# Seven products of quarter sums for eight in two blocks of a two-layer float32 network on one Trainium2 core

## The chip, the cores and the metric

One core of one Trainium2 chip runs the whole program. The metric is the device time of one execution in microseconds, as the median of several runs. TensorE's clock was granted at full speed in every slice of the profile.

## The reference

An attention block with 32 state rows per head gives 2,176 rows of 512 numbers (17 tiles of 128 rows). Two expert layers follow, each of the form `g(x @ w_in) @ w_out` with widths 512, 2,048 and 512, all in float32:

```python
def _moe2_ref(x, w_in, w_out):
    h = x @ w_in
    sp = np.where(h > 20.0, h, np.log1p(np.exp(np.minimum(h, 20.0))))
    g = h * np.tanh(sp)
    return (g @ w_out).astype(np.float32)
```

The first layer has ELU in place of this function. The change concerns the second layer's last line, `g @ w_out`.

## The kernel before

**Products.** A float32 operand is split into a high part in the fast float32 format of TensorE and a low part that holds the rest. Each product is then three matmuls into one accumulator: high by high, high by low, low by high (lines 872 to 874 in the first product of a layer, 972 to 974 in the second). Each matmul loads its own 128x128 stationary operand and streams up to 512 columns.

**Steps.** The work is a list of steps. In the second layer, BLOCKS2 (line 39) makes five blocks of 4, 4, 4, 3 and 2 tiles; a block has 16 steps, one for each slice j of 128 of the 2,048 hidden columns. In a step of a block of four tiles `mm1` (line 839) issues 12 matmuls of 512 columns into one PSUM bank of the tag `h`, which has four banks (SPOTS). `hidden` (line 884) turns that bank into g on ScalarE and VectorE: Exp, a bound, a product, Ln, Exp, two products (lines 919 to 931), then the split into a high part by ScalarE and a low part by VectorE (`split_g`, line 934). Two steps later `mm2` (line 940) multiplies the four tiles of g by the slice of `w_out`, 12 matmuls of 512 columns, into the four banks acc0 to acc3, which add up over the 16 steps. `retire` (line 983) copies the accumulators out and stores them. The last two blocks ("narrow", line 1116) issue four steps of `mm1` and then four of `mm2`.

**Order.** Every instruction is added to a plan with a cost and due times from a table T of step starts (line 347). `Plan.run` (line 126) simulates the engines and always issues what can start first, ties going to what is due first; the result is a fixed order for each engine. A transfer is issued by SP's queue, in the order that the plan gave. Buffers come from pools of named tags with a fixed number of buffers, among them `w_out` (16), `wraw` (3), `o` (4), `e`, `g`, `u` and `ms` (2 each).

**Weights.** `weight` (line 460) brings the second layer's weights from 64-bit words to float32 and parks them in DRAM (w2d). `reload` (line 522) fetches them again and `split_weight` (line 515) splits them into the 16 `w_in` and 16 `w_out` buffers, where they stay for all five blocks. `fold_slice` (line 564) and the first layer are not touched.

Of the kernel before, what the change touches and what calls it, by code (L numbers as in the profile page):

```python
# [235 lines left out]
def attention_elu_mish(  # L236
# [41 lines left out]
    s2d = pools["dram"].tile([B, 2, P, S], F32, name="s2d")  # L278
    at = ctx.enter_context(ExitStack())
# [61 lines left out]
    def mm2_cost(kind, n, whole=False):  # L341
        return 4 * mm(4 * S) if whole else 12 * mm(n * P if kind == 1 else DM)
# [5 lines left out]
    for s, (kind, blk, t0, n, j) in enumerate(steps):  # L348
        c = mm1_cost(kind, blk, n, j) + (mm2_cost(kind, n, whole_out(kind, blk, j)) if kind < 2 else n * 3 * mm(DM))
        T.append(T[-1] + c + (PACE_FIRST if s < NF // 2 else PACE if s < first2 else 0.0))  # L350
# [171 lines left out]
    def reload(kind, j):  # L522
        v = buf("work", "wraw", 3, [P, DM], F32, f"back_{kind}_{j}_")
        add(SP, 256.0, lambda: nc.sync.dma_start(out=v.t, in_=w2d[:, kind == "out", j, :]),
            r=[("w2d", kind, j)], w=[v])
        split_weight(kind, 2, j, v)


# [355 lines left out]
    def hidden(s, h):  # L884

        kind, blk, t0, n, j = steps[s]
        e = buf("work", "e", EBUFS, [P, MAXN])
# [19 lines left out]
        if apart(s):  # L907
            g = buf("l2", "g", 2, [P, 2, n * P], F32R, "g")
        else:
            g = buf("work", "g", GBUFS, [P, 2, MAXN], F32R, "g")  # L910
        gs[s] = g
        last = s == len(steps) - 1
        g.parts = [(0, n // 2), (n // 2, n)] if last else [(0, n)]
        sw = switch
        for q, (c0, c1) in enumerate(g.parts):
# [16 lines left out]
            split_g(g, e, c0 * P, c1 * P, [ke], q)  # L932
# [7 lines left out]
    def mm2(s, only=None):  # L940
        kind, blk, t0, n, j = steps[s]
        g = gs[s]
        part = (kind, blk)
# [161 lines left out]
    for j in range(NF):  # L1105
        begin(index[1, 3, j], reload, "in", j)
        begin(min(index[1, 3, j] + 1, first2), reload, "out", j)
    for blk in range(len(BLOCKS2)):
        begin(first2 + NF * (blk - 1) + 6 if blk else s_state + NQ + 4, load_x2, blk)
# [8 lines left out]
    for s in range(len(steps) + 2):  # L1118
# [13 lines left out]
        if s < len(steps) and s >= narrow and (s - narrow) % GROUP < GROUP - 1:  # L1132
            held.append(s - 2)
            continue
# [55 lines left out]
SPOTS = 4  # L1190
WARM, EARLY, XB, EBUFS, GBUFS, FOLD_LAG = 14, 8, 3, 2, 2, 3.0
# [25 lines left out]
```

## Time and profile before

| | |
|---|---|
| median of 3 runs | 714.25 us (714.08 to 714.56) |
| the profiled execution's own time | 714.31 us |
| its span in the profile | 712.4 us |
| TensorE busy | 706.3 us of the span, 4,082 matmuls |
| VectorE busy | 526.1 us |
| ScalarE busy | 411.6 us |
| DMA | 81.50 MB, 114 GB/s on the mean |

PE is TensorE's matmul side, PEld its weight loads, DVE is VectorE, ACT ScalarE, SP the queue that issues transfers. Matmuls are pipelined, so that the duration of one is longer than the distance to the next: the pace is read from start times. Neighbouring instructions of VectorE and of ScalarE overlap a little in the same way. L972 is line 972 of the kernel.

### The profile page before, as it was taken

To read this page: it belongs to the slowest core of one execution; us is meant where nothing else is said; L and a number is where in the kernel's file an instruction comes from. 1 tells how busy PE (TensorE), PEld (TensorE's weight loads), DVE (VectorE), ACT (ScalarE), POOL (GpSimd) and SP (SyncE) were. 2 spreads that over 40 slices of the span, in tenths; PEclk is the share of its full clock that TensorE was granted. 3 is DMA by queue.
4 is the path that set the end of the run, shared out by engine and by line. 5 is a ranking of instruction groups with operands and counts; after the bars stand their busy time and mean duration, and the time that the engine had idled before them with its cause. 6 is when DMAs were issued, how large, how long until landed. Compare 5 with 4: busy or idle time off the path is not lost.

```text
span 712.4 us, 10844 instructions
## 1 busy us (share of the span) xinstructions
PE 706.3 (99%) x4082; PEld 583.2 (82%) x4082; DVE 526.1 (74%) x1004; ACT 411.6 (58%) x735; POOL 11.8 (2%) x26
## 2 busy tenths in 40 slices
PE   8999999999999999999999999999999999999998
PEld 7578777878888898788888888888888889999887
DVE  7999998879797846887888566666666647665575
ACT  4987775656666734565666455544545436554464
POOL 1000000100000000000000000000000000000000
PEclk9999999999999999999999999999999999999999
DMA  9846788364788835636860003000030000200100
GB/s 288 292 148 194 221 212 218 95 143 105 239 218 256 262 104 169 203 120 193 261 225 13 1 0 119 0 1 1 2 102 1 1 1 1 88 1 1 45 1 30
DMA packets 89895, 81.50 MB, mean 114 GB/s; under 512 B 46452, under 2 KB 68980, under 8 KB 89844
## 3 DMA queue, kind: packets, MB, share of 16 engines
q1 hardware_dynamic: 89428, 80.63, 37.9%
q8 instruction: 32, 0.52, 0.3%
q10 hardware_dynamic: 416, 0.20, 0.1%
q14 instruction: 19, 0.16, 0.1%
HBM read 59.31 MB, written 21.50 MB: 113 GB/s over the span
## 4 chain that ended last, share of the span: by engine, by line
PE 97%; DMA 1%; ACT 1%; DVE 0%; issue 0%; SPq 0%; DVEq 0%; ACTq 0%
PE acc_acc L972 17%; PE acc_acc L973 17%; PE acc_acc L974 17%; PE h L872 13%; PE h L873 13%; PE h L874 13%; PE fold L551 2%; PE h L848 2%; PE h L858 1%; DMA raw_in<-in_moe_w_in 1%; PE sr L796 1%; PE acc_acc L960 1%; PE acc_h L973 1%; PE acc_h L974 1%; PE acc_h L972 1%; PE warm L385 0%
## 5 line engine op out<-in xcount | busy, mean ns | idle before, releaser
L936 ACT CAST g<-e 128x512 fp32r<-128x512 f32 (+3 forms) x148 | 86.2, 582 | 119.9 <-DVE e L930 63.2
L937 DVE TENSOR_TENSOR g<-e,g 128x512 fp32r<-128x512 f32 (+3 forms) x148 | 95.1, 644 | 49.2 <-ACT g L936 48.1
L874 PE MATMUL h<-x,w_in 128*128 128x512 f32 (+2 forms) x320 | 114.2, 357 | 0.0
L873 PE MATMUL h<-x,w_in 128*128 128x512 f32 (+2 forms) x320 | 114.2, 357 | 0.0
L872 PE MATMUL h<-x,w_in 128*128 128x512 f32 (+2 forms) x320 | 114.2, 357 | 0.0
L972 PE MATMUL acc_acc<-w_out,g 128*128 128x512 f32 x272 | 106.0, 390 | 0.0
L973 PE MATMUL acc_acc<-w_out,g 128*128 128x512 f32 x272 | 105.9, 390 | 0.0
L974 PE MATMUL acc_acc<-w_out,g 128*128 128x512 f32 x272 | 105.9, 389 | 0.0
L972 PE MATMUL acc_acc<-g,w_out 128*128 128x512 f32 x252 | 100.2, 398 | 0.0
L973 PE MATMUL acc_acc<-g,w_out 128*128 128x512 f32 x252 | 98.2, 390 | 0.0
L974 PE MATMUL acc_acc<-g,w_out 128*128 128x512 f32 x252 | 98.1, 389 | 0.0
L924 ACT ACTIVATE e<-u,two 128x512 f32<-128x512 f32 (+3 forms) x81 | 53.0, 655 | 64.3 <-DVE u L922 64.1
L928 DVE TENSOR_TENSOR u<-u,e 128x512 f32<-128x512 f32 (+3 forms) x81 | 48.9, 605 | 53.6 <-ACT e L926 53.2
L919 ACT ACTIVATE e<-h 128x512 f32<-128x512 f32 (+3 forms) x81 | 42.7, 529 | 45.8 <-PE h L874 37.4
L872 PEld LDWEIGHTS h<-x,w_in 128*128 128x128 f32 x320 | 60.3, 189 | 7.8
L873 PEld LDWEIGHTS h<-x,w_in 128*128 128x128 f32 x320 | 60.3, 189 | 7.7
L874 PEld LDWEIGHTS h<-x,w_in 128*128 128x128 f32 x320 | 60.3, 188 | 7.5
L972 PEld LDWEIGHTS acc_acc<-w_out,g 128*128 128x128 f32 x272 | 51.1, 188 | 11.0 <-ACT o L294 0.5
L974 PEld LDWEIGHTS acc_acc<-w_out,g 128*128 128x128 f32 x272 | 51.1, 188 | 10.7
L891 ACT ACTIVATE e<-h 128x512 f32<-128x512 f32 x68 | 40.2, 595 | 33.7 <-PE h L874 22.4
L973 PEld LDWEIGHTS acc_acc<-w_out,g 128*128 128x128 f32 x272 | 51.1, 188 | 10.2
L920 DVE TENSOR_SCALAR e<-e 128x512 f32<-128x512 f32 (+3 forms) x81 | 31.0, 383 | 36.8 <-ACT e L919 36.0
(149 smaller groups left out, 1125.8 us busy)
## 6 DMA issues: line engine op xcount, KB each, us to landing
raw_in<-in_moe_w_in SPq DMA_DIRECT2D x32, 512.0 KB, 5.1
raw_out<-in_moe_w_out SPq DMA_DIRECT2D x32, 512.0 KB, 4.0
w2d<-wv SPq DMA_DIRECT2D x32, 256.0 KB, 3.3
x2d<-o SPq DMA_DIRECT2D x16, 256.0 KB, 3.5
xb<-in_x SPq DMA_DIRECT2D x32, 128.0 KB, 4.4
back_in<-w2d SPq DMA_DIRECT2D x16, 256.0 KB, 3.3
back_out<-w2d SPq DMA_DIRECT2D x16, 256.0 KB, 3.0
out<-o SPq DMA_DIRECT2D x15, 256.0 KB, 2.1
```

The costliest lines, as they stand in the source:

```text
L872: nc.tensor.matmul(h[:, :n], lhsT=wh, rhs=xh, start=(k == 0), stop=False)
L873: nc.tensor.matmul(h[:, :n], lhsT=wh, rhs=xl, start=False, stop=False)
L874: nc.tensor.matmul(h[:, :n], lhsT=wl, rhs=xh, start=False, stop=(k == nk - 1))
L891: add("ACT", act(n), lambda: nc.scalar.activation(E(), Hh(), AF.Exp), r=[h], w=[e])
L919: add("ACT", act(n), lambda c=c: nc.scalar.activation(e[:, c], h[:, c], AF.Exp), r=[h], w=[ke])
L924: add("ACT", act(n) + 0.1, lambda c=c: nc.scalar.activation(e[:, c], u[:, c], AF.Ln, bias=two), r=[ku, "two"], w=[ke])
L928: add("DVE", dve(n), lambda c=c: nc.vector.tensor_tensor(u[:, c], u[:, c], e[:, c], ALU.mult), r=[ku, ke], w=[ku])
L936: add("ACT", act(n), lambda: nc.scalar.copy(g[:, 0, c], e[:, c]), r=r, w=[(g, 0, q)])
L937: add("DVE", dve(n), lambda: nc.vector.tensor_tensor(g[:, 1, c], e[:, c], g[:, 0, c].bitcast(F32), ALU.subtract), r=[*r, (g, 0, q)], w=[(g ...
L972: nc.tensor.matmul(acc.t, lhsT=st[:, 0, :], rhs=mv[:, 0, :], start=fst, stop=False)
L973: nc.tensor.matmul(acc.t, lhsT=st[:, 0, :], rhs=mv[:, 1, :], start=False, stop=False)
L974: nc.tensor.matmul(acc.t, lhsT=st[:, 1, :], rhs=mv[:, 0, :], start=False, stop=lst)
```

## The change

In blocks 1 and 2 of the second layer (`SEVEN`) two neighbouring slices j of the hidden columns make a pair, eight pairs to a block. g of the pair (512 rows by 256 columns) and the two slices of `w_out` (256 by 512) are each cut into four quarters, and the 2x2 product of quarters is made in seven products of sums of quarters. One product is 6 matmuls of 256 columns; its accumulator fills a bank of its own through the eight pairs: acc0 to acc3 and three of the four banks of `h`.

- `hidden` copies the bank of `h` to SBUF first (ScalarE), and reads the copy from then on.
- `g_sums` makes four sums of quarters of g on VectorE for each pair, and splits seven widths of 256 columns where the pair had four.
- `make_factors` makes the sums of quarters of `w_out` before block 1 and parks them in DRAM (f2d); `reload` parks the split slices of `w_out` (h2d); `load_factors` loads four operands for each pair into the 16 `w_out` buffers, which the operands of g share; `halves_back` loads the 16 slices again for blocks 3 and 4.
- `seven_products` issues two of the seven products after `mm1` of the next step and five after the one behind it. At a block's end it copies seven banks out, and `result_sums` forms the four quarters of the result with seven additions over the next steps.

```diff
@@ -276,6 +276,8 @@
...
     s2d = pools["dram"].tile([B, 2, P, S], F32, name="s2d")
+    f2d = pools["dram"].tile([P, NF // 2, 2, 2, DM], F32, name="f2d")
+    h2d = pools["dram"].tile([P, NF, 2, DM], F32, name="h2d")
     at = ctx.enter_context(ExitStack())
     pools["at"] = at.enter_context(tc.tile_pool(name="attn", bufs=1))
@@ -346,7 +348,8 @@
     T = [START]
     for s, (kind, blk, t0, n, j) in enumerate(steps):
-        c = mm1_cost(kind, blk, n, j) + (mm2_cost(kind, n, whole_out(kind, blk, j)) if kind < 2 else n * 3 * mm(DM))
+        c = mm1_cost(kind, blk, n, j) + (mm2_cost(kind, n, whole_out(kind, blk, j)) if kind < 2 else
+                                         (30 if j % 2 else 12) * mm(HALF_E) if blk in SEVEN else n * 3 * mm(DM))
         T.append(T[-1] + c + (PACE_FIRST if s < NF // 2 else PACE if s < first2 else 0.0))
     T += [T[-1] + 3.0 * i for i in range(1, 4)]
@@ -524,7 +527,67 @@
         add(SP, 256.0, lambda: nc.sync.dma_start(out=v.t, in_=w2d[:, kind == "out", j, :]),
             r=[("w2d", kind, j)], w=[v])
         split_weight(kind, 2, j, v)
-
+        if kind == "out":
+            w = w_sb[kind, 2, j]
+            add(SP, 512.0, lambda: nc.sync.dma_start(out=h2d[:, j], in_=w.t.bitcast(F32)),
+                r=[(w, 0), (w, 1)], w=[("h2d", j)])
+    def halves_back(j):
+        w = w_sb["out", 2, j] = buf("w", "w_out", NF, [P, 2, DM], F32R, f"w_again{j}_")
+        add(SP, 512.0, lambda: nc.sync.dma_start(out=w.t.bitcast(F32), in_=h2d[:, j]), r=[("h2d", j)],
+            w=[(w, 0), (w, 1)], after=[products[max(products) - (j < NF // 2)][FREED[j % 8]]], lag=2.0)
+    last_lo = []
+    def make_factors(p, due):
+        done = []
+        v = buf("work", "wraw", 3, [P, 2, DM], F32, f"quarters{p}_")
+        for i in range(2):
+            add(SP, 256.0, lambda i=i: nc.sync.dma_start(out=v[:, i], in_=w2d[:, 1, 2 * p + i, :]),
+                r=[("w2d", "out", 2 * p + i)], w=[(v, i)])
+        t = [buf("work", "o", OBUFS, [P, DM], F32, f"sum{p}_{i}_") for i in range(2)]
+        lo, hi = slice(0, HALF_E), slice(HALF_E, DM)
...
+        for k, (o, a, b) in enumerate((("T1", "B12", "B11"), ("T2", "B22", "T1"),
+                                       ("T3", "B22", "B12"), ("T4", "T2", "B21"))):
+            add("DVE", dve(HALF_E), lambda o=parts[o][0], a=parts[a][0], b=parts[b][0]: nc.vector.tensor_tensor(
+                o(), a(), b(), ALU.subtract), r=[parts[a][1], parts[b][1]], w=[parts[o][1]], place=t if not k else (), due=due, after=last_lo)
+        for i, (u, r) in enumerate(((lambda: t[0].t, [(t[0], 0), (t[0], 1)]), (lambda: t[1].t, [(t[1], 0), (t[1], 1)]))):
+            n = DM
+            f = [buf("work", tag, 2, [P, n], F32R, f"f{p}_{i}_") for tag in ("wv", "wy")]
+            add(EITHER, {"ACT": act(n), "DVE": 0.34 * n / DM}, lambda e, f=f, u=u: copy(e, f[0].t, u()),
+                r=r, w=[f[0]], due=due)
+            add("DVE", dve(n), lambda f=f, u=u: nc.vector.tensor_tensor(
+                f[1].t, u(), f[0].t.bitcast(F32), ALU.subtract), r=[*r, f[0]], w=[f[1]], due=due)
+            done.append(plan.ops[-1])
+            for k in range(2):
+                add(SP, n / 2, lambda f=f, i=i, n=n, k=k: nc.sync.dma_start(
+                    out=f2d[:, p, i, k, :n], in_=f[k].t.bitcast(F32)), r=[f[k]], w=[("f2d", p, i, k)], due=due)
...
+    factors = {}
+    def factor(p, i):
+        n = DM if i < 3 else HALF_E
+        return buf("w", "w_out", NF, [P, 2, n], F32R, f"f{p}_{i}_")
+    def load_factors(blk, p):
+        made = []
+        for i in range(4):
+            f, n = factor(p, i), DM if i < 3 else HALF_E
+            prev = products.get(8 * blk + p - 2, {})
+            src, names = (f2d[:, p, i], [("f2d", p, i, k) for k in range(2)]) if i < 2 else                 (h2d[:, 2 * p + 3 - i, :, :n], [("h2d", 2 * p + 3 - i)])
+            add(SP, n, lambda f=f, src=src: nc.sync.dma_start(out=f.t.bitcast(F32), in_=src), r=names, w=[(f, 0), (f, 1)], after=[prev[k] for k in USERS[i] if prev], lag=2.0)
+            made.append(f)
+        factors[blk, p] = made
+    products = {}
     m_sb = {}
@@ -884,7 +947,8 @@
     def hidden(s, h):
         kind, blk, t0, n, j = steps[s]
-        e = buf("work", "e", EBUFS, [P, MAXN])
+        seven = kind == 2 and blk in SEVEN
+        e = buf("work", "ms", 2, [P, MAXN], F32, "e") if seven and not j % 2 else buf("work", "e", EBUFS, [P, MAXN])
         if kind < 2:
             n *= P
             E, Hh = (lambda: e.t), (lambda: h.t)
@@ -904,15 +968,23 @@
             split_g(g, e, 0, n, [e])
             return
         u = buf("l2", "u", 2, [P, MAXN])
-        if apart(s):
+        g = None
+        if seven or kind == 2 and s - index[2, max(SEVEN), NF - 1] in COPIED:
+            ps, h = h, buf("work", "wraw", 3, [P, MAXN], F32, "hs")
+            add("ACT", act(n * P), lambda n=n: nc.scalar.copy(h[:, :n * P], ps[:, :n * P]), r=[ps], w=[h])
+        if seven:
+            pass
+        elif apart(s):
             g = buf("l2", "g", 2, [P, 2, n * P], F32R, "g")
         else:
             g = buf("work", "g", GBUFS, [P, 2, MAXN], F32R, "g")
         gs[s] = g
         last = s == len(steps) - 1
-        g.parts = [(0, n // 2), (n // 2, n)] if last else [(0, n)]
+        parts = [(0, n // 2), (n // 2, n)] if last else [(0, n)]
+        if g:
+            g.parts = parts
         sw = switch
-        for q, (c0, c1) in enumerate(g.parts):
+        for q, (c0, c1) in enumerate(parts):
             n = (c1 - c0) * P
             c = slice(c0 * P, c1 * P)
             ke, ku = (e, q), (u, q)
@@ -929,7 +1001,97 @@
                 r=[ku, ke], w=[ku])
             add("DVE", dve(n), lambda c=c: nc.vector.tensor_tensor(e[:, c], h[:, c], u[:, c], ALU.mult),
                 r=[h, ku], w=[ke])
-            split_g(g, e, c0 * P, c1 * P, [ke], q)
+            if seven:
+                g_sums(s, e, ke)
+            else:
+                split_g(g, e, c0 * P, c1 * P, [ke], q)
+    evens, g_factors = {}, {}
+    def g_sums(s, e, ke):
+        kind, blk, t0, n, j = steps[s]
+        p = 8 * blk + j // 2
+        lo, hi = slice(0, HALF_E), slice(HALF_E, DM)
+        prev = products.get(p - 2)
+        def sub(o, ko, a, ka, b, kb, op=ALU.subtract):
+            behind = [(gs[s - 1], 1, 0)] if gs.get(s - 1) else []
+            add("DVE", dve(HALF_E), lambda: nc.vector.tensor_tensor(o(), a(), b(), op), r=[ka, kb],
+                after=[plan.writer[k] for k in behind], w=[ko])
+        def split(v, r, i, c):
+            g, n = parts[i], c.stop - c.start
+            add("ACT", act(n), lambda: nc.scalar.copy(g[:, 0, c], v()), r=r, w=[(g, 0, c.start)],
+                after=[prev[k] for k in GUSERS[i]] if prev else ())
+            add("DVE", dve(n), lambda: nc.vector.tensor_tensor(
+                g[:, 1, c], v(), g[:, 0, c].bitcast(F32), ALU.subtract), r=r + [(g, 0, c.start)], w=[(g, 1, c.start)])
+        if not j % 2:
+            parts = g_factors[p] = [buf("w", "w_out", NF, [P, 2, DM if i < 3 else HALF_E], F32R, f"g{p}_{i}_")
+                                    for i in range(4)]
+            t = buf("work", "g", GBUFS, [P, 2, MAXN], F32, "gsum")
+            evens[p] = e, ke, t
+            sub(lambda: t[:, 1, lo], (t, 1, 0), lambda: e[:, lo], ke, lambda: e[:, hi], ke)
+            split(lambda: e[:, lo], [ke], 0, lo)
+            split(lambda: t[:, 1, lo], [(t, 1, 0)], 0, hi)
+            return
+        parts = g_factors[p]
+        f, kf, t = evens.pop(p)
+        split(lambda: e.t, [ke], 1, slice(0, DM))
+        sub(lambda: t[:, 0, lo], (t, 0, 0), lambda: f[:, hi], kf, lambda: e[:, hi], ke, ALU.add)
+        sub(lambda: t[:, 0, hi], (t, 0, 1), lambda: t[:, 0, lo], (t, 0, 0), lambda: f[:, lo], kf)
+        split(lambda: t[:, 0], [(t, 0, 0), (t, 0, 1)], 2, slice(0, DM))
+        sub(lambda: t[:, 1, hi], (t, 1, 1), lambda: e[:, lo], ke, lambda: t[:, 0, hi], (t, 0, 1))
+        split(lambda: t[:, 1, hi], [(t, 1, 1)], 3, lo)
+    def seven_products(s):
+        kind, blk, t0, n, j = steps[s]
+        p = j // 2
+        pp = 8 * blk + p
+        if not p:
+            accs[kind, blk] = {k: spot(tag, f"m{blk}_{k}_") for k, tag in SEVEN_BANKS.items()}
+        acc, g, f = accs[kind, blk], g_factors.pop(pp), factors.pop((blk, p))
+        made = products[pp] = {}
+        for o, k in enumerate(SEVEN_ORDER):
+            gi, gc, fi, fc = OPERANDS[k]
+            gk, fk = [(g[gi], h, 0 if gi == 1 else gc * HALF_E if gi == 0 else 0) for h in range(2)], \
+                [(f[fi], h) for h in range(2)]
+            def run(a=acc[k], g=g[gi], gc=gc, f=f[fi], fc=fc):
+                for q in range(2):
+                    c, w = slice(gc * HALF_E + q * P, gc * HALF_E + (q + 1) * P), slice(fc * HALF_E, (fc + 1) * HALF_E)
+                    out = a[:, q * HALF_E:(q + 1) * HALF_E]
+                    nc.tensor.matmul(out, lhsT=g[:, 0, c], rhs=f[:, 0, w], start=not p and not q, stop=False)
+                    nc.tensor.matmul(out, lhsT=g[:, 0, c], rhs=f[:, 1, w], start=False, stop=False)
+                    nc.tensor.matmul(out, lhsT=g[:, 1, c], rhs=f[:, 0, w], start=False, stop=p == NF // 2 - 1 and q == 1)
+            made[k] = add("PE", 6 * mm(HALF_E), run, r=gk + fk, w=[acc[k]],
+                          due=T[s + 1 + (o >= 2)] + SEVEN_DUE + 0.5 * o)
+        if p < NF // 2 - 1:
+            return
+        due = T[s + 2] + 2.0
+        o = {c: buf("work", "o", OBUFS, [P, DM], F32, f"o{blk}_{c}_") for c in ("11", "12", "21", "22")}
+        first, second, third = (buf("work", tag, 2, [P, DM], F32, f"u_{tag}_") for tag in ("wv", "wv", "wy"))
+        v = {1: first, 6: second, 7: third, 2: o["11"], 3: o["12"], 4: o["21"], 5: o["22"]}
+        for i, k in enumerate(SEVEN_ORDER):
+            add(EITHER, both(DM), lambda e, k=k: copy(e, v[k].t, acc[k].t), r=[acc[k]], w=[v[k]],
+                due=due + 0.5 * i + LATE_COPY)
+        for i, sums in enumerate(SUMS):
+            begin(s + SUMS_AT[i], result_sums, sums, v, t0)
+    def result_sums(sums, v, t0):
+        for to, a, b, op in sums:
+            add("DVE", 0.605, lambda to=to, a=a, b=b, op=op: nc.vector.tensor_tensor(
+                v[to].t, v[a].t, v[b].t, getattr(ALU, op)), r=[v[a], v[b]], w=[v[to]])
+            if to in RESULTS:
+                i, e = RESULTS[to]
+                for q in range(2):
+                    add(SP, 128.0, lambda to=to, q=q, t=t0 + 2 * i + q, e=e: nc.sync.dma_start(
+                        out=out_rows(t)[..., e * HALF_E:(e + 1) * HALF_E],
+                        in_=v[to][:, q * HALF_E:(q + 1) * HALF_E]), r=[v[to]], due=T[len(steps)])
     def split_g(g, e, c0, c1, r, q=0):
         n, c = c1 - c0, slice(c0, c1)
@@ -940,6 +1102,10 @@
     def mm2(s, only=None):
         kind, blk, t0, n, j = steps[s]
         g = gs[s]
+        if kind == 2 and blk in SEVEN:
+            if j % 2:
+                seven_products(s)
+            return list(products[max(products)].values()) if products else []
         part = (kind, blk)
         if part not in accs:
             tags = ["h"] if kind == 0 else [f"acc{i}" for i in range(NK if kind == 1 else n)]
@@ -1105,6 +1271,14 @@
     for j in range(NF):
         begin(index[1, 3, j], reload, "in", j)
         begin(min(index[1, 3, j] + 1, first2), reload, "out", j)
+        begin(index[2, max(SEVEN), NF - 1] + 1 + j // 4, halves_back, j)
+    for p in range(NF // 2):
+        g = index[2, min(SEVEN) - 1, 0] + FACTORS_FROM + int(p * FACTORS_STEP)
+        begin(g, make_factors, p, T[g + FACTORS_TO])
+    for blk in sorted(SEVEN):
+        for p in range(NF // 2):
+            begin(index[2, blk, 0] + 2 * p if blk > min(SEVEN) or p > 1 else index[2, blk, 0] - 4 + 2 * p,
+                  load_factors, blk, p)
...
@@ -1129,7 +1303,8 @@
                 f(*args)
             gate[:] = []
             hidden(s, h)
-        if s < len(steps) and s >= narrow and (s - narrow) % GROUP < GROUP - 1:
+        if s < len(steps) and s >= narrow and (s - narrow) % GROUP < GROUP - 1 and \
+                not (steps[s - 2][0] == 2 and steps[s - 2][1] in SEVEN):
             held.append(s - 2)
             continue
         if s == len(steps):
@@ -1162,8 +1337,11 @@
 WHOLE_J = 4
...
+HALF_E = DM // 2
+SEVEN = {1, 2}
...
+FACTORS_FROM, FACTORS_STEP, FACTORS_TO = -18, 2.3, 20
...
+OPERANDS = {1: (0, 0, 3, 0), 2: (1, 0, 2, 0), 3: (3, 0, 2, 1), 4: (1, 1, 1, 1), 5: (2, 0, 0, 0), 6: (2, 1, 0, 1),
+            7: (0, 1, 1, 0)}
+USERS = {i: [k for k, v in OPERANDS.items() if v[2] == i] for i in range(4)}
+GUSERS = {i: [k for k, v in OPERANDS.items() if v[0] == i] for i in range(4)}
+SEVEN_ORDER = (1, 7, 2, 4, 5, 6, 3)
+FREED = (1, 7, 4, 4, 6, 6, 3, 3)
+COPIED = (1,)
+LATE_COPY = 0.0
+SEVEN_DUE = 0.0
+SUMS = (((6, 1, 6, "add"),), ((2, 1, 2, "add"),), ((7, 6, 7, "add"),), ((4, 7, 4, "subtract"),), ((6, 6, 5, "add"),),
+        ((5, 7, 5, "add"),), ((3, 6, 3, "add"),))
+RESULTS = {2: (0, 0), 3: (0, 1), 4: (1, 0), 5: (1, 1)}
+SUMS_AT = (6, 7, 9, 11, 13, 14, 15)
+SEVEN_BANKS = {1: "acc0", 7: "acc1", 2: "acc2", 4: "acc3", 5: "h", 6: "h", 3: "h"}
...
```

## Rows read from the trace of the kernel before

**Rows 1.** The page of the profile: the span, and its parts 1 and 2.

```profile
span 712.4 us, 10844 instructions
...
PE 706.3 (99%) x4082; PEld 583.2 (82%) x4082; DVE 526.1 (74%) x1004; ACT 411.6 (58%) x735; POOL 11.8 (2%) x26
...
PEclk9999999999999999999999999999999999999999
```

**Rows 2.** Stretches: one early, the steps before layer 2, its blocks 0, 1, 2.

```profile
core 0: us, PE busy (x) PEld busy (x) DVE busy (x) ACT busy (x) POOL busy (x), PEclk, DMA share, GB/s
60.00:80.00 20.00, 20.00 (x145) 15.86 (x144) 19.32 (x38) 15.44 (x28) 1.77 (x2) 1.00 0.90 263
260.00:330.80 70.80, 70.80 (x419) 59.84 (x418) 52.63 (x102) 40.57 (x68) 0.00 (x0) 1.00 0.50 155
330.80:417.80 87.00, 87.00 (x385) 72.07 (x384) 67.03 (x116) 49.28 (x81) 0.00 (x0) 1.00 0.37 119
417.80:504.90 87.10, 87.10 (x386) 72.09 (x386) 54.75 (x88) 43.04 (x69) 0.00 (x0) 1.00 0.08 25
504.90:591.90 87.00, 87.00 (x385) 72.06 (x384) 50.73 (x83) 40.64 (x66) 0.00 (x0) 1.00 0.08 22
```

**Rows 3.** TensorE in order of time, block 1: starts of mm1, mm2, next mm1.

```profile
417.84 0.39 PE L872 MATMUL h<-x,w_in 128*128 128x512 f32 x1
...
420.56 0.39 PE L972 MATMUL acc_acc<-w_out,g 128*128 128x512 f32 x1
...
423.28 0.39 PE L872 MATMUL h<-x,w_in 128*128 128x512 f32 x1
```

**Rows 4.** TensorE in the last block: 48 matmuls of 256 columns, 24 of 512, again.

```profile
672.45 0.28 PE L872 MATMUL h<-x,w_in 128*128 128x256 f32 x1
...
678.21 0.40 PE L972 MATMUL acc_acc<-w_out,g 128*128 128x512 f32 x1
...
683.67 0.28 PE L872 MATMUL h<-x,w_in 128*128 128x256 f32 x1
```

**Rows 5.** ScalarE and VectorE in order of time, one step's chain in block 1.

```profile
415.32 0.60 ACT L919 ACTIVATE e<-h 128x512 f32<-128x512 f32 x1
...
419.29 0.69 DVE L930 TENSOR_TENSOR e<-h,u 128x512 f32<-128x512 f32 x1
...
420.07 0.62 ACT L936 CAST g<-e 128x512 fp32r<-128x512 f32 x1 [1.54 <-DVE e L930]
420.72 0.69 DVE L937 TENSOR_TENSOR g<-e,g 128x512 fp32r<-128x512 f32 x1 [0.74 <-ACT g L936]
420.76 0.60 ACT L919 ACTIVATE e<-h 128x512 f32<-128x512 f32 x1
```

**Rows 6.** Around a bank's copy at 669 us: ScalarE's copy, TensorE waiting for it.

```profile
668.93 0.57 ACT L294 COPY o<-acc_acc 128x512 f32<-128x512 f32 x1
...
669.12 0.39 PE L974 MATMUL acc_acc<-w_out,g 128*128 128x512 f32 x1
...
669.55 0.19 PEld L972 LDWEIGHTS acc_acc<-w_out,g 128*128 128x128 f32 x1 [0.47 <-ACT o L294]
```

**Rows 7.** ScalarE, then VectorE, in order of time: instructions independent of one another.

```profile
66.12 0.59 ACT L891 ACTIVATE e<-h 128x512 f32<-128x512 f32 x1
66.65 0.41 ACT L294 CAST ms<-m 128x256 fp32r<-128x256 f32 x1
66.96 0.72 ACT L893 ACTIVATE e<-e,one 128x512 f32<-128x512 f32 x1
67.58 0.66 ACT L485 ACTIVATE wy<-raw_in 128x512 f32<-128x512 f32 x1
...
62.43 0.42 DVE L572 TENSOR_TENSOR ms<-m,ms 128x256 fp32r<-128x256 f32 x1
62.77 0.68 DVE L294 COPY o<-acc_acc 128x512 f32<-128x512 f32 x1
63.37 0.68 DVE L900 SCALAR_TENSOR_TENSOR e<-e,h 128x512 f32<-128x512 f32 x1
```

**Rows 8.** Transfers: the tile back_out on SP's queue; raw_out, time to landing.

```profile
L524 SPq DMA_DIRECT2D back_out<-w2d x16: 319/320/391, 249.1 to 372.6; - x16
...
raw_out<-in_moe_w_out SPq DMA_DIRECT2D x32, 512.0 KB, 4.0
```

More of the change, by code (lines that the diff above doesn't have):

```diff
@@ new lines, in attention_elu_mish @@
+    last_lo = []
[7 more added lines that the diff above has]
+        lo, hi = slice(0, HALF_E), slice(HALF_E, DM)
+        parts = {"B11": (lambda: v[:, 0, lo], (v, 0)), "B12": (lambda: v[:, 0, hi], (v, 0)),
+                 "B21": (lambda: v[:, 1, lo], (v, 1)), "B22": (lambda: v[:, 1, hi], (v, 1)),
+                 "T1": (lambda: t[0][:, lo], (t[0], 0)), "T2": (lambda: t[0][:, hi], (t[0], 1)),
+                 "T3": (lambda: t[1][:, lo], (t[1], 0)), "T4": (lambda: t[1][:, hi], (t[1], 1))}
+        for k, (o, a, b) in enumerate((("T1", "B12", "B11"), ("T2", "B22", "T1"),
[13 more added lines that the diff above has]
+                    out=f2d[:, p, i, k, :n], in_=f[k].t.bitcast(F32)), r=[f[k]], w=[("f2d", p, i, k)], due=due)
+        last_lo[:] = done
```

## The prediction

> **What bounds the kernel now.** I read the page's busy times first: TensorE works in 706.3 of 712.4 us, at a granted clock of 9 tenths or more in every slice [rows 1]. Busy matmuls overlap, so this share alone doesn't prove a bound. The table of stretches does better: in blocks 0, 1 and 2 of the second layer TensorE fills 87.00 of 87.00, 87.10 of 87.10 and 87.00 of 87.00 us, while VectorE has 67.03, 54.75 and 50.73, ScalarE 49.28, 43.04 and 40.64, and DMA falls to 25 and 22 GB/s [rows 2]. Then the order in time gives TensorE's pace: one step is 12 matmuls of `mm1` in 420.56 - 417.84 = 2.72 us and 12 of `mm2` in 2.72 us, so 5.44 / 24 = 0.2267 us for one of 512 columns, with no gap [rows 3]. The last block shows the other width that matters: 48 matmuls of 256 columns, each with its own weight load, take 678.21 - 672.45 = 5.76 us, 0.120 each, and the 24 of 512 columns that follow take 5.46 [rows 4]. So TensorE's instruction stream is the bound, and only what it issues, or a wait put into it, can move the time.
>
> The profiled execution took 714.31 us, its span of 712.4 and 1.91 around it; the sum is made against it. The median, 714.25, is 0.06 lower, which I neglect.
>
> **The product, on the path.** For each pair the change removes 24 matmuls of 512 columns, 5.44 us, and adds 7 x 6 = 42 of 256 columns, the shape of rows 4: 42 x 0.120 = 5.04. A run of 512 columns after one of 256 is slower by 5.46 - 5.44 = 0.02 us [rows 3, 4]; each pair has two such changes of width, 0.04. That saves 0.36 us for each pair, and 16 pairs save 5.8 us. Only 6 of 48 half-width matmuls go, an eighth, but the narrow ones are dearer: 2 x 0.120 - 0.2267 = 0.013 us stays the same for any width, and 18 more matmuls for each pair pay it, 0.24 us. The product breaks even at 5.44 / 42 = 0.1295 us for a narrow matmul. I take the measured 0.120. The ends: columns alone would price it at half of 0.2267, 0.113, and save 10.9 us; at 0.125, midway to break-even, it saves 2.4.
>
> The Trainium skill's page "TensorE: Matmul & The Clock Gate" (section "Wait — 56ns, not 53.3ns?") has a smaller fixed cost, 2.5 ns for each matmul; my estimate from that page is that the change would save 9.5 us. The rows here contradict it with 13 ns.
>
> **One bank of `h`, a new wait.** Three of its four banks become accumulators. `mm1` of the next step must now wait until ScalarE has copied the only bank left. After the even step TensorE has 12 narrow matmuls to do meanwhile, 1.44 us; after the odd one 30, 3.6 us. The price of the hand-over: ScalarE begins 420.76 - 420.56 = 0.20 us after the matmuls [rows 3, 5]; a copy out of PSUM lasts 0.57 and TensorE went on 669.55 - 669.50 = 0.05 us after it [rows 6], 0.82 in all. So 0.62 us of cover remain behind the even step. ScalarE works in order, and an instruction ahead of the copy costs 0.53 (66.12 to 66.65) to 0.62 (66.96 to 67.58) [rows 7]: one just fits, two make TensorE 0.53 to 0.62 late. Where the plan sees this it can issue the next product of the older pair first. I take nothing for it; the ends are 0 and 16 x 0.53 = 8.5 us. Behind the waiting `mm1` stand all later products, since TensorE's order is fixed.
>
> **The chain to g.** It gets longer by the copy, some 0.6 us, and by the sums. Before, the last elementwise result is ready 420.07 - 415.32 = 4.75 us after Exp starts [rows 5], so some 5.6 us after `mm1`. In the even step a sum and two splits follow, about 1.5 us: 7.1, where the first product needs it 1.44 + 2.72 + 3.6 + 2.72 = 10.5 us after `mm1`. In the odd step the last operand needs three sums and two splits, 3 to 4 us: up to 9.6, needed at about 13.4. Three to four microseconds of cover each; nothing on the path.
>
> **VectorE and ScalarE.** Each pair adds 4 sums and 3 low parts of 256 columns on VectorE, 0.34 us each where they don't wait for one another (62.43 to 62.77; 512 columns 0.60) [rows 7]: 56 x 0.34 = 19 us for each block; the block's end adds 7 additions and at most 3 more copies, 6 us. Block 1 gets to 54.75 + 25 = 80, block 2 to 76, in a block shortened to about 84 us. That is tight, but early in the kernel VectorE is busy 19.32 of 20 us and TensorE 20.00 of 20 [rows 2]. ScalarE gets two copies and three high parts more for each pair, 2 x 0.53 + 3 x 0.31 = 2.0 us, 16 for each block, and stays under 60. The operand sums of `w_out` (four of 256 columns, two copies and two low parts of 512 for each pair, about 8 x 3.2 = 26 us if VectorE makes them all) may spread from 18 steps ahead of block 0 into block 1; VectorE has 18 us free there before block 0 and 20 in it [rows 2]. They are due late, so they fill gaps. Without that cover they would cost what doesn't fit, a few microseconds.
>
> **Transfers and SP.** Parking 16 split slices, reading 16 and writing 32 quarters' operands moves 21 MB, to the 155 x 70.8 + 119 x 87 = 21 MB of the same stretch [rows 2]: 42 MB in 158 us, 270 GB/s if none of it fell later, against the 263 seen at a share of 0.90. The writes are due late and come behind the reloads that block 0 needs. In blocks 1 and 2 a pair loads 1.84 MB in 10.5 us, 175 GB/s; the load is released 10.5 us ahead of its first product, and 512 KB land in 4.0 us [rows 8]. SP gets some 150 more issues of 0.32 us [rows 8], 49 us over 330; behind one that waits stand only transfers due later. I take nothing; the end is a few microseconds at a block's start.
>
> **Ends of blocks.** The seven copies run under the next step's `mm1`; the additions and stores fall 6 to 15 steps later, far ahead of the kernel's end. From block 2 to 3 the third `mm1` needs a copied bank with 1.44 us of cover against 0.82; I allow 0.3 us, here and at the entry of block 1 together.
>
> **Sum.** -5.8 + 0.3 = -5.5: 714.31 - 5.5 = 708.8 us.
>
> **Rivals.**
> *Half of it is given back at the single bank.* In half of the pairs two ScalarE instructions stand ahead of the copy: 8 x 0.53 = 4.3 us, 713.1. For it: ScalarE gets more to do, and the cover is 0.62 us. Against it: ScalarE is free 40% of the time, and the plan sees the wait. The Trainium skill's "Perfetto Trace Analysis" (section "Optimizing Tensor Performance") asks that independent groups of matmuls rotate through different PSUM banks so that a copy overlaps the next group; by that rule this is the place to lose time. Its chance is 0.13.
>
> *VectorE becomes the bound; slower.* Place: blocks 1 and 2. If the 66 added instructions pay their full durations, 0.42 and 0.69 us, and 0.09 between an instruction and the next engine (419.29 + 0.69 to 420.07) [rows 5, 7], a block gets 56 x 0.42 + 10 x 0.69 + 66 x 0.09 = 36.4 us more: 91.2 us in block 1 and 87.1 in block 2, against 87.1 and 87.0 now, so 718.5. It decides from 87.1 - 54.75 = 32 us of added work, 0.49 for each. For it: the sums depend on one another. Against it: independent work stands beside them, and rows 7 show 0.34. Chance 0.10.
>
> *The fixed share doesn't count.* In long runs of narrow matmuls it would be hidden: 18 x 0.013 more for each pair, 3.7 us, 705.1. This is the side on which the page on TensorE stands. Rows 4 are such a run and show it paid: 0.03.
>
> *Nothing comes of it.* The reordered plan loses elsewhere, at the reloads for block 0, what the product saves: 714, chance 0.05, bounded by the transfers above.
>
> **Numbers.** The forecast has 0.69. About 0.2%, 1.4 us, is what a measurement of this kernel can tell from no change. Faster: the forecast, the hidden share and the 0.08 of the first rival in which fewer than half of the pairs are late, 0.80; the same: 0.08, from the first and the last rival; slower: 0.12, VectorE and some 0.02 for a bank that is late in every pair. The range reaches from 707.3 (the product without changes of width and at 0.119) to 713.2, which takes in the first rival at its price; left out are VectorE as the bound, the hidden share and larger losses, 0.2.
>
> **What would show it.** TensorE has 16 x 18 = 288 more matmuls. Runs of 12 and 30 narrow matmuls at 0.120 us stand between the `mm1` of blocks 1 and 2; two steps last 10.5 us in place of 10.9; block 3 starts 5.5 us earlier. VectorE is busy around nine tenths in these blocks with TensorE still full. Waits of TensorE for ScalarE's copy at the second `mm1` of a pair, 0.5 us each, would show the first rival; TensorE waiting for VectorE's low parts, at the products, the second; a narrow pace of 0.13 would void the sum.

## The result and the profile after

The kernel with seven products takes **708.12 us** in the median (707.95 to 708.67, 4 runs) against 714.16 beside it (713.90 to 714.56): 6.04 us less, a ratio of 0.9916, 95% interval 0.9899 to 0.9933. The profiled execution took 707.95 us, 1.85 more than its span.

The page of the kernel after, its span and busy times, which answer to [rows 1]:

```profile
span 706.1 us, 12109 instructions
...
PE 701.0 (99%) x4370; PEld 592.5 (84%) x4370; DVE 584.5 (83%) x1176; ACT 452.9 (64%) x840; POOL 12.0 (2%) x26
```

TensorE has 288 matmuls more and is busy 5.3 us less: 672 narrow ones stand in the place of 384 wide ones. VectorE is busy 58 us longer and ScalarE 41, and neither shows in the time. The stretches of the kernel after, to be held against [rows 2]: the steps before layer 2, its block 0, then the two changed blocks:

```profile
core 0: us, PE busy (x) PEld busy (x) DVE busy (x) ACT busy (x) POOL busy (x), PEclk, DMA share, GB/s
260.00:330.80 70.80, 70.80 (x419) 59.93 (x419) 54.91 (x108) 43.65 (x74) 0.00 (x0) 1.00 0.73 250
330.80:417.80 87.00, 87.00 (x386) 72.06 (x385) 76.11 (x142) 53.01 (x89) 0.00 (x0) 1.00 0.83 282
417.80:502.00 84.20, 84.20 (x510) 75.55 (x509) 70.43 (x143) 56.59 (x107) 0.00 (x0) 1.00 0.62 205
502.00:586.00 84.00, 84.00 (x529) 76.13 (x529) 75.12 (x153) 58.85 (x113) 0.00 (x0) 1.00 0.59 191
```

Look at the second number of each line, TensorE's busy time: it still fills every stretch, although VectorE rises from 54.75 and 50.73 us to 70 and 75, and DMA from 25 and 22 GB/s to about 200. Every wait of TensorE that the profile lists (engine, line, what it waited for: total, times, longest) is at the kernel's start:

```profile
PE warm L388 <- DVE ident_col L362: 1.1, 1, 1.1
PE st L444 <- DVE st_raw L296: 0.4, 1, 0.4
```

TensorE in order of time over the second pair's steps, which answers to [rows 3] and [rows 4] (L935 first product, L1066 the seven products):

```profile
430.94 0.28 PE L1066 MATMUL m<-f,g 128*128 128x256 f32 x1
...
432.37 0.40 PE L935 MATMUL h<-x,w_in 128*128 128x512 f32 x1
...
435.12 0.28 PE L1066 MATMUL m<-f,g 128*128 128x256 f32 x1
...
438.71 0.40 PE L935 MATMUL h<-x,w_in 128*128 128x512 f32 x1
...
441.46 0.28 PE L1066 MATMUL m<-f,g 128*128 128x256 f32 x1
```

12 narrow matmuls take 1.43 us, 30 take 3.59 (0.1197 each), a first product between narrow runs 2.75 in place of 2.72. A pair takes 441.46 - 430.94 = 10.52 us where two steps took 10.88: 0.36 us less, and all pairs of both blocks show the same figures (the last one's first products are block 3's, of 384 columns). 16 x 0.36 = 5.8 us. The other 0.5 us between the two spans lies ahead of layer 2, which begins at 330.80 us in the trace before and at 330.30 in this one. 0.33 of it is there by 40 us, ahead of anything changed, and is variation: layer 2 begins at 329.97 to 331.07 in the profiles of the variants below, and at 332.96 in one. Some 0.17 us come at 234 us, where the new plan puts the same matmuls in another order.

### The profile page after: what moved, and what is told of

Its sections match the earlier page's. It is cut to its first block, busy times and chain, and to the rows that moved or that the text cites. A ratio compares the mean times of both kernels' runs of the same rounds, so it can differ in the third digit from the quotient of the medians.

```text
span 706.1 us, 12109 instructions
## 1 busy us (share of the span) xinstructions
PE 701.0 (99%) x4370; PEld 592.5 (84%) x4370; DVE 584.5 (83%) x1176; ACT 452.9 (64%) x840; POOL 12.0 (2%) x26
## 4 chain that ended last, share of the span: by engine, by line
PE 97%; DVE 1%; ACT 1%; DMA 1%; SPq 0%; issue 0%
PE acc_acc L1138 13%; PE h L935 13%; PE h L936 13%; PE h L937 13%; PE acc_acc L1140 13%; PE acc_acc L1139 13%; PE m L1068 4%; PE m L1067 4%; PE m L1066 4%; PE fold L614 2%; PE h L911 2%; PE h L921 1%; DMA st_raw<-in_state 1%; PE sr L859 1%; PE acc_acc L1126 1%; PE acc_h L1138 1%
## 5 line engine op out<-in xcount | busy, mean ns | idle before, releaser
L935 PE MATMUL h<-x,w_in 128*128 128x512 f32 (+2 forms) x320 | 114.6, 358 | 0.0
L936 PE MATMUL h<-x,w_in 128*128 128x512 f32 (+2 forms) x320 | 114.6, 358 | 0.0
L1098 ACT CAST g<-e 128x512 fp32r<-128x512 f32 (+3 forms) x116 | 66.3, 572 | 68.1 <-PE acc_acc L1140 35.7
L1099 DVE TENSOR_TENSOR g<-e,g 128x512 fp32r<-128x512 f32 (+3 forms) x116 | 72.9, 629 | 23.3 <-ACT g L1098 22.3
L935 PEld LDWEIGHTS h<-x,w_in 128*128 128x128 f32 x320 | 60.5, 189 | 7.0
L936 PEld LDWEIGHTS h<-x,w_in 128*128 128x128 f32 x320 | 60.5, 189 | 6.7
L1068 PE MATMUL m<-f,g 128*128 128x256 f32 x224 | 63.4, 283 | 0.0
L1067 PE MATMUL m<-f,g 128*128 128x256 f32 x224 | 63.4, 283 | 0.0
L1066 PE MATMUL m<-f,g 128*128 128x256 f32 x224 | 63.2, 282 | 0.0
L1138 PEld LDWEIGHTS acc_acc<-g,w_out 128*128 128x128 f32 x252 | 47.4, 188 | 12.8 <-issue 1.7
L1140 PEld LDWEIGHTS acc_acc<-g,w_out 128*128 128x128 f32 x252 | 47.3, 188 | 10.0
L1139 PEld LDWEIGHTS acc_acc<-g,w_out 128*128 128x128 f32 x252 | 47.3, 188 | 9.8 <-issue 0.5
L964 DVE SCALAR_TENSOR_TENSOR e<-e,h 128x512 f32<-128x512 f32 x67 | 45.5, 680 | 10.7 <-ACT e L957 10.6
```

Of the source, the lines that this page charges most:

```text
L935: nc.tensor.matmul(h[:, :n], lhsT=wh, rhs=xh, start=(k == 0), stop=False)
L936: nc.tensor.matmul(h[:, :n], lhsT=wh, rhs=xl, start=False, stop=False)
L1066: nc.tensor.matmul(out, lhsT=g[:, 0, c], rhs=f[:, 0, w], start=not p and not q, stop=False)
L1067: nc.tensor.matmul(out, lhsT=g[:, 0, c], rhs=f[:, 1, w], start=False, stop=False)
L1068: nc.tensor.matmul(out, lhsT=g[:, 1, c], rhs=f[:, 0, w], start=False, stop=p == NF // 2 - 1 and q == 1)
L1098: add("ACT", act(n), lambda: nc.scalar.copy(g[:, 0, c], e[:, c]), r=r, w=[(g, 0, q)])
```

## The experiments

Each is an edit of the kernel after. A variant with lines more has line numbers one or two higher: L936 in it can be the first product's L935.

**One block alone.** The saving is tested for its proportion, and for a cost of entering and leaving the scheme.

```diff
-SEVEN = {1, 2}
+SEVEN = {1}
```

> Seven products in block 1 alone; block 2 has its eight again. If the end is set by what TensorE issues, eight pairs save 8 x 0.36 = 2.9 us and the time is about 711.3 us, half of the way from 714.2 to 708.1. If entering and leaving the scheme costs something once (copies, loads, the reload of w_out), one block saves less than half, 712 or more.

```diff
-SEVEN = {1, 2}
+SEVEN = {2}
```

> Seven products in block 2 alone. By the same theory 711.3 us. If block 1 owed its gain, or a loss, to the operand sums of w_out that are still made while it runs, this block and block 1 alone would differ by more than 0.5 us.

Measured: 711.63 us for block 1 (ratio 0.9960, 0.9947 to 0.9972) and 711.20 for block 2 (0.9956, 0.9942 to 0.9970), against 714.37 of the kernel before, measured beside them: 2.7 and 3.2 us less. The sum, 5.9, is the whole change's 6.0 within the noise. No entrance cost and no difference of 0.5 us between the blocks is visible. In the two profiles layer 2, from its first matmul's start to its last one's, is 2.90 and 2.98 us shorter than before: both blocks save 8 x 0.36.

**Eight narrow products.** The narrow matmul is priced by itself, with all sums, copies and loads left in place.

```diff
...
-            made[k] = add("PE", 6 * mm(HALF_E), run, r=gk + fk, w=[acc[k]],
...
+            twice = k == 4
+            made[k] = add("PE", (12 if twice else 6) * mm(HALF_E), (lambda run=run: (run(last=False), run(first=False))) if twice else run,
...
```

> One of the seven products (number 4) is issued twice in every pair, so that 48 narrow matmuls stand where there were 42; sums, copies and loads stay as they are. The result counts that product twice. If TensorE's instructions set the time, 16 pairs pay 16 x 6 x 0.12 = 11.5 us more: 719.6 us, which is 5.5 us slower than the kernel before, since 48 narrow matmuls cost more than 24 wide ones. If TensorE had been waiting for sums or operands, part of it would be free, 712 to 717.

Measured: 719.63 us, 11.5 above 708.12, and a ratio of 1.0073 (1.0054 to 1.0091) to the kernel before. So 96 narrow matmuls cost their full 0.12 us each, with nothing free beside them. It also settles where the gain is from: eight products at this width are slower than the kernel before by 5.3 us (719.63 against 714.37 beside it), and the 11.5 us of the product left out have to pay for that first.

**No cover for the copy of the bank.** The hand-over of the bank, from TensorE to ScalarE's copy and back, is laid bare: all seven products come after the odd step's first product, so that TensorE has no cover, that is no other matmuls to do meanwhile.

```diff
-                          due=T[s + 1 + (o >= 2)] + SEVEN_DUE + 0.5 * o)
+                          due=T[s + 1 + (o >= 0)] + SEVEN_DUE + 0.5 * o, after=latest if o >= 0 else ())
...
-            turn = first = [plan.ops[-1]]
+            turn = first = latest = [plan.ops[-1]]
...
```

> All seven products are held back until the first product of the odd step has been issued, so nothing covers the copy of the single bank behind the even step. The theory of the hand-over prices this at 0.82 us for each pair, 16 x 0.82 = 13.1, less 0.03 for one change of width fewer: about 720.7 us. If an instruction of ScalarE usually stands ahead of the copy, 1.35 us for each pair, 729.

Measured: 721.90 us, 13.8 above 708.12. What TensorE waited for in the blocks of this variant, in the same columns as above, and one hand-over in order of time:

```profile
PE h L935 <- ACT hs L974: 9.9, 14, 0.9
```

```profile
440.88 0.39 PE L937 MATMUL h<-x,w_in 128*128 128x512 f32 x1
...
441.38 0.58 ACT L974 COPY hs<-h 128x512 f32<-128x512 f32 x1
...
442.01 0.50 PE L935 MATMUL h<-x,w_in 128*128 128x512 f32 x1 [0.74 <-ACT hs L974]
...
442.35 0.40 PE L936 MATMUL h<-x,w_in 128*128 128x512 f32 x1
```

The first product's last matmul has streamed by 440.88 + 0.23 = 441.11. TensorE starts again at 442.01, 0.05 us after the copy, a wait of 0.90 (the profile counts 0.74, from the end that it models for the matmul). The next start is at 442.35, 0.34 later and not 0.23: a start after a wait costs another 0.11. Two first products in a row take 6.44 us in 8 of 13 pairs of this trace, up to 6.65 in the others, and 5.47 in one without a wait: 0.97 or more for each hand-over. 14 of them make at least 13.6 of the 13.8 us. The expectation had 16 at 0.82, without the slow start.

**Half of the cover.** One product between the two first products.

```diff
-                          due=T[s + 1 + (o >= 2)] + SEVEN_DUE + 0.5 * o)
+                          due=T[s + 1 + (o >= 1)] + SEVEN_DUE + 0.5 * o, after=latest if o >= 1 else ())
...
-            turn = first = [plan.ops[-1]]
+            turn = first = latest = [plan.ops[-1]]
...
```

> One product stands between the two first products of a pair and six after them: 6 x 0.12 = 0.72 us of cover for the single bank's copy in place of 1.44. By the hand-over of 0.82 us each pair waits 0.1 us, 709.7 us. If an instruction of ScalarE stands ahead of the copy in half of the pairs, 0.53 to 0.62 us more there: 714.

Measured: 711.90 us (711.14 to 717.51, 10 runs), ratio 0.9980 (0.9963 to 0.9998), 3.8 above 708.12: between the two expectations. TensorE around one hand-over:

```profile
441.45 0.28 PE L1066 MATMUL m<-f,g 128*128 128x256 f32 x1
...
442.04 0.28 PE L1068 MATMUL m<-f,g 128*128 128x256 f32 x1
442.29 0.50 PE L935 MATMUL h<-x,w_in 128*128 128x512 f32 x1
442.62 0.39 PE L936 MATMUL h<-x,w_in 128*128 128x512 f32 x1
```

The narrow run ends at 442.04 + 0.12 = 442.16; the wait is 0.13, the start after it 0.33 instead of 0.23. That is 0.24 us for each of 14 pairs, 3.4 us. The hand-over, from 441.45 to 442.29, is 0.84 us, and no other instruction of ScalarE stands in it; the expectation lacked the 0.1 us of the new start.

**One and two instructions of ScalarE more in the hand-over.** This is the rival of the single bank, made to happen.

```diff
-            add("ACT", act(n * P), lambda n=n: nc.scalar.copy(h[:, :n * P], ps[:, :n * P]), r=[ps], w=[h])
+            for _ in range(2 if seven and not j % 2 else 1):
+                add("ACT", act(n * P), lambda n=n: nc.scalar.copy(h[:, :n * P], ps[:, :n * P]), r=[ps], w=[h])
```

> The copy of the bank of h is made twice in the even steps, so that one more instruction of ScalarE, about 0.5 us, stands ahead of TensorE's next first product: 0.20 + 0.5 + 0.57 + 0.05 = 1.3 us against 1.44 of cover. By the hand-over's price nothing is lost, 708.1 us. If ScalarE usually has something else ahead of the copy too, some pairs wait, up to 16 x 0.5 = 8 us.

The second variant has 3 in place of 2.

> Three copies in the even steps: 1.8 us against 1.44 of cover, 0.4 us late in each pair, and 0.11 more for the start after a wait, as the run without cover showed: 16 x 0.5 = 8 us, 716 us. If the plan sees the delay in its own order and puts an older pair's product into the gap, as it can, less: 709 to 711, since only changes of width are added.

Measured: 713.30 us with two copies (712.80 to 719.25, 10 runs; ratio 0.9996, 0.9979 to 1.0013) and 719.82 with three (1.0081, 1.0066 to 1.0096). The first lies between its two expectations, the second above both of its own. ScalarE and TensorE in the variant with two copies, around one hand-over:

```profile
484.38 0.59 ACT L975 COPY hs<-h 128x512 f32<-128x512 f32 x1 [1.12 <-PE h L937]
484.86 0.62 ACT L1026 CAST g<-e 128x512 fp32r<-128x512 f32 x1
485.38 0.59 ACT L975 COPY hs<-h 128x512 f32<-128x512 f32 x1
...
486.02 0.50 PE L935 MATMUL h<-x,w_in 128*128 128x512 f32 x1 [0.25 <-ACT hs L975]
```

In this plan the split of g went between the two copies, so the hand-over has two instructions more and not one: 0.41 us late and 0.11 for the new start, 0.52 in 9 of the 16 pairs. In the kernel after, the first copy is the only one, and the split comes behind it. With three copies, in the worst hand-over (ScalarE from 509.88 us on), a split and a copy of an accumulator stand between them, and TensorE is 1.56 us late; where the plan puts a third product in front of the next first product, as at 463.58, it is still 0.2 us late.

**Without the copy.**

```diff
-        if seven or kind == 2 and s - index[2, max(SEVEN), NF - 1] in COPIED:
+        if kind == 2 and s - index[2, max(SEVEN), NF - 1] in COPIED:
```

> The copy of the bank of h is left out in blocks 1 and 2 and the steps read PSUM as before. The single bank is then free only after the last elementwise product has read it, 4.86 us after the matmuls, plus 0.05. The cover is 1.44 us behind the even step and 3.6 behind the odd one: 3.5 + 1.3 = 4.8 us for each pair, 16 x 4.8 = 77 us, about 785 us. If the plan's order could hide it, well under 740.

Measured: 788.81 us in one run, 80.7 above 708.12. TensorE's first wait, the columns as before:

```profile
PE h L935 <- DVE e L1002: 53.4, 25, 3.8
```

L1002 is the last product that reads `h`. A wait behind an even step, and a stretch soon after it:

```profile
453.19 0.28 PE L1068 MATMUL m<-f,g 128*128 128x256 f32 x1
456.79 0.51 PE L935 MATMUL h<-x,w_in 128*128 128x512 f32 x1 [3.31 <-DVE e L1002]
458.50:460.50 2.00, 2.00 (x6) 1.55 (x5) 1.03 (x3) 0.40 (x1) 0.00 (x0) 0.50 0.03 8
```

TensorE stands still from 453.19 + 0.12 to 456.79, 3.48 us; behind odd steps it is 1.3. Both are as expected, 3.5 and 1.3. That the total came out near 785 is in part luck: there are 25 such waits and not 32, 57 us. Some 17 us more are 88 matmuls at the granted clock of 0.50, the lower level of 1.2 GHz, which follows the long waits, and 3 are slow starts. A single bank is affordable here only through the copy.

**More work for VectorE.** The sums of quarters of g are made twice: all four of a pair, then the even step's alone.

```diff
-            add("DVE", dve(HALF_E), lambda: nc.vector.tensor_tensor(o(), a(), b(), op), r=[ka, kb],
-                after=[plan.writer[k] for k in behind], w=[ko])
+            for _ in range(2):
+                add("DVE", dve(HALF_E), lambda: nc.vector.tensor_tensor(o(), a(), b(), op), r=[ka, kb],
+                    after=[plan.writer[k] for k in behind], w=[ko])
```

> Each of the four sums of quarters of g is made twice, with the same result: 8 x 4 x 0.34 = 10.9 us more of VectorE for each block, in which it is busy 70 and 75 of 84 us. If VectorE is next in line, block 2 gets to 86 of 84 us and the time rises by 2 us or more, 710 to 712. If the gaps still hold it, 708.1.

The second variant has `range(1 if j % 2 else 2)`.

> Only the even step's sum is made twice: one instruction of 256 columns more for each pair, 8 x 0.34 = 2.7 us more of VectorE for each block, against 10.9 in the run that made all four twice and cost 8.8 us. If VectorE still has gaps to give, TensorE stays full and the time is 708.1 us. If it has none left, a quarter of that cost, 710.3.

Measured: 716.90 us with all four (715.41 to 723.40, 9 runs; ratio 1.0046, 1.0023 to 1.0069), and 708.24 with one (0.9917, 0.9901 to 0.9934). What TensorE waited for with all four, beside the start:

```profile
PE m L1069 <- DVE g L1028: 3.2, 4, 2.1
PE h L935 <- ACT hs L974: 1.4, 2, 0.8
```

Stretches of blocks 1 and 2, first with one sum doubled, then with all four:

```profile
430.00:513.00 83.00, 83.00 (x525) 75.34 (x524) 71.56 (x149) 58.83 (x110) 0.00 (x0) 1.00 0.63 196
513.00:586.00 73.00, 73.00 (x461) 66.22 (x460) 65.75 (x139) 51.21 (x97) 0.00 (x0) 1.00 0.59 192
```

```profile
430.00:513.00 83.00, 81.77 (x506) 73.17 (x504) 76.62 (x166) 55.64 (x105) 0.00 (x0) 1.00 0.61 196
513.00:586.00 73.00, 71.52 (x438) 63.95 (x439) 69.36 (x152) 51.34 (x95) 0.00 (x0) 1.00 0.53 171
```

2.7 us more in a block (by the price of 0.34; against the kernel after the busy times of the two stretches rise by 1.1 and 0.7 us) are free, and 10.9 (6.2 and 4.3) are not: VectorE at 86 to 90% of a stretch leaves TensorE full, at 92 to 95% it doesn't. So VectorE's work is next in line, and the room in front of it is between 2.7 and 10.9 us in a block. TensorE waits there for low parts of g (L1028), and around its longest wait VectorE is busy 2.00 of 2.00 us (the last table below). These runs don't separate how much of that is VectorE having no time left and how much the chain of sums to g that the doubling lengthens.

**More transfers.** All four operands of `w_out` are loaded twice, then two of four.

```diff
-            add(SP, n, lambda f=f, src=src: nc.sync.dma_start(out=f.t.bitcast(F32), in_=src), r=names, w=[(f, 0), (f, 1)], after=[prev[k] for k in USERS[i] if prev], lag=2.0)
+            for _ in range(2):
+                add(SP, n, lambda f=f, src=src: nc.sync.dma_start(out=f.t.bitcast(F32), in_=src), r=names, w=[(f, 0), (f, 1)], after=[prev[k] for k in USERS[i] if prev], lag=2.0)
```

> Each operand of w_out is loaded twice into its buffer: 3.67 MB for each pair in 10.5 us, 350 GB/s, where the busiest slice of the profile has 365 and the stretch over block 0 282. If the loads have little room, TensorE waits for them, at 300 GB/s by 1.7 us for each pair: up to 735 us. If they are well hidden, 708.1.

The second variant has `range(2 if i < 2 else 1)`.

> Two of the four operands of w_out are loaded twice into their buffers: 2.88 MB for each pair in 10.5 us, 274 GB/s in place of 175. If the room of the loads ends between this and the 350 GB/s that cost 13 us, TensorE stays full and the time is 708.1 us. If any added transfer delays the products, about half of that cost, 715.

Measured: 721.47 us with four (1.0103, 1.0083 to 1.0123) and 710.90 with two (710.88 to 713.81; 0.9954, 0.9937 to 0.9970). Block 1 of each, four and then two, in the columns of the stretches:

```profile
430.00:513.00 83.00, 78.59 (x483) 68.99 (x482) 66.53 (x134) 53.88 (x102) 0.00 (x0) 1.00 0.96 342
```

```profile
430.00:513.00 83.00, 83.00 (x504) 73.67 (x503) 69.07 (x141) 54.97 (x104) 0.00 (x0) 1.00 0.81 289
```

With four, the DMA engines are busy 0.96 of the time. The only wait that the profile lists for TensorE in these blocks is again for the bank's copy:

```profile
PE h L936 <- ACT hs L975: 9.3, 13, 0.9
```

In this plan's order the next first product comes directly behind the even step's. 13 hand-overs, each 0.74 to 1.08 us late and 0.11 more for the slow start, make 12.8 us of the 13.2 by which layer 2 is longer than in the kernel after. So it is the order that costs 13 us. That the plan chose it because it expected late operands is likely and not shown; whether these loads would be late in the order of the kernel after, no run shows.

With two, no wait is listed in these blocks. The profile is of the slowest of four executions, 713.81 us, whose layer 2 begins 2.7 us late, at 332.96; from there on it is 3.1 us longer than the kernel after. One hand-over:

```profile
466.04 0.28 PE L1069 MATMUL m<-f,g 128*128 128x256 f32 x1
466.28 0.50 PE L936 MATMUL h<-x,w_in 128*128 128x512 f32 x1
466.62 0.40 PE L937 MATMUL h<-x,w_in 128*128 128x512 f32 x1
```

The plan cuts first products into pieces of 3 and 6 matmuls and leaves one product behind the even step, so that 11 hand-overs are 0.12 us late or more and pay for the slow start, 2.7 of the 3.1 us. The real load of about 200 GB/s thus has room: 289 GB/s delayed no operand that TensorE is listed as waiting for.

## Why the prediction was right

**The product.** The prediction took 42 x 0.120 + 0.04 us for a pair; the trace has 1.43 + 3.59 = 5.02 us of narrow matmuls and 0.03 us on each of two first products, 5.08 in sum. The saving of 0.36 us for each pair is the measured one. The lower end, columns alone (its 10.9 us leave out the changes of width, with them 10.2), is refuted by the narrow runs at 0.1197, and with it the third rival: the fixed share is 2 x 0.1197 - 0.2267 = 0.0127 us, paid in full. What the Trainium skill's page "TensorE: Matmul & The Clock Gate" (section "Wait — 56ns, not 53.3ns?") gives, 2.5 ns, doesn't hold for these matmuls.

**The single bank.** Priced at 0.82 us against 1.44 of cover. The line of ScalarE in the kernel after, in the third pair:

```profile
452.18 0.59 ACT L974 COPY hs<-h 128x512 f32<-128x512 f32 x1 [1.21 <-PE h L937]
```

ScalarE has been idle for 1.21 us when the bank is done; the copy starts 0.20 us after the last matmul (451.98) and ends at 452.77, 0.64 ahead of the first product at 453.41. With the 0.05 of the return, 0.59 us of room remain, where the prediction had 0.62; in the 15 even steps from 430.94 on the figures are the same each time. So nothing is lost here, because nothing stands in front of the copy, and not by a wide margin. Where the bank is late, the prediction's price was too low: it lacked the 0.11 us of the slow start. By its own numbers two instructions ahead make TensorE 2 x 0.53 - 0.62 = 0.44 to 0.62 us late, not 0.53 to 0.62; with two copies it is 0.41, and 0.11 on top. The variants put prices to the first rival: 3.8 us for half of the cover, 5.2 for one more copy, 13.8 with no cover.

**The chain to g.** This step was too hopeful, though nothing came of it. The prediction had the even step's operand of g ready 7.1 us after its first product, with 3 to 4 us to spare. The last low part of g for one pair, and the product that reads it:

```profile
440.94 0.42 DVE L1027 TENSOR_TENSOR g<-gsum,g 128x256 fp32r<-128x256 f32 x1
442.17 0.28 PE L1066 MATMUL m<-f,g 128*128 128x256 f32 x1
```

It is ready at 441.36, 10.4 us after its first product has streamed (430.94) and 0.8 us ahead of its use. Over the 16 pairs this room is 0.8 to 2.3 us. The prediction added up durations and left out that each instruction also waits behind other steps' on ScalarE and VectorE. With all four sums doubled it is here that TensorE waits first.

**VectorE.** Estimated at 80 and 76 us of some 84; found at 70 and 75 in the stretches, which are cut a little differently. The second rival needed 32 us of added work in a block; the stretches show 15.7 and 24.4. Its condition is nearer than that: with 10.9 us more by the price, VectorE is busy 92 to 95% of the stretches, not full on the mean, and TensorE loses time.

**The ends of the blocks.** The prediction allowed 0.3 us. Nothing was lost: the first product of block 3 follows block 2 without a wait, and the single blocks sum to the whole. This, and 0.3 to 0.5 us ahead of layer 2, of which most is variation, is the difference between 708.8 and 708.12.

**The transfers.** 250 and 282 GB/s ahead of block 1, about 200 in the two blocks; taken as hidden, and hidden: the profile lists no wait of TensorE for them, and over block 0 TensorE is busy 87.00 of 87.00 us as before. So the last rival, a loss at the reloads, did not come.

## What to carry to other kernels

Seven products for eight save an eighth of the columns, not of the time: the narrower matmuls pay their fixed share more often, and here only 0.36 of 5.44 us was left. Price the narrow shape from a row that has it before building the sums. When accumulators take the banks away, an early copy to SBUF makes one bank do, if independent matmuls of about 0.9 us stand behind the product (the hand-over measured 0.84) and nothing stands in front of the copy on its engine. And read from the trace, not from a sum of durations, how long before its use an operand is ready.

## What the runs showed that was not expected

A wait of TensorE costs about 0.11 us beyond itself: the matmul after it starts its successor 0.33 to 0.34 us later and not 0.23. The weight loads (PEld) around the hand-over with half of the cover, whose matmuls start at 441.45, 442.29 and 442.62:

```profile
441.22 0.19 PEld L1066 LDWEIGHTS m<-f,g 128*128 128x128 f32 x1
...
442.28 0.19 PEld L935 LDWEIGHTS h<-x,w_in 128*128 128x128 f32 x1 [0.17 <-ACT hs L974]
...
442.39 0.19 PEld L936 LDWEIGHTS h<-x,w_in 128*128 128x128 f32 x1
```

Without a wait the load starts 0.23 us ahead of its matmul; after one it starts with it, so that the load is no longer covered. That this is the whole cause is a reading of the trace; no run changed it alone. The Trainium skill's page "TensorE: Matmul & The Clock Gate" (section "LDWEIGHTS (loading the stationary operand)") gives a load the number of columns / 1.2 in ns; my estimate from it is 107 ns for 128 columns. The trace agrees in that the next load starts 0.11 us later, though it lists each load with 0.19. Short waits are nearly doubled by it: 0.13 us became 0.24.

A long wait costs the clock as well. Stretches of the run with all four sums doubled, around the end of block 2, columns as above:

```profile
589.00:591.00 2.00, 0.48 (x4) 0.27 (x3) 2.00 (x6) 1.18 (x4) 0.00 (x0) 1.00 1.04 369
591.00:593.00 2.00, 1.46 (x7) 1.46 (x8) 2.00 (x5) 1.27 (x2) 0.00 (x0) 0.64 0.98 383
593.00:595.00 2.00, 2.00 (x11) 2.00 (x11) 1.99 (x6) 1.02 (x2) 0.00 (x0) 0.51 0.47 191
595.00:597.00 2.00, 2.00 (x14) 2.00 (x14) 1.90 (x5) 0.00 (x0) 0.00 (x0) 1.00 0.89 240
```

After one wait of 2.1 us for VectorE the granted clock is 0.51, the lower of its two levels, 1.2 GHz, while TensorE is busy 2.00 of 2.00 us; then it is back. The 14 narrow matmuls from 591.92 on start every 0.213 us in place of 0.120, 1.3 us more in sum. The times say the same: the two of the nine executions with a mean granted clock of 1.000 took 715.41 and 715.64 us, the six at 0.997 or 0.998 took 716.70 to 717.39, and one at 0.990 took 723.40. That is part of why the doubled sums cost 8.8 us where the listed waits sum to 4.6.
